# Token matmuls of one class in 64-lane pairs, and a new order in the head of a spectral and gated-GELU kernel

## The chip, the core and the metric

The kernel runs on one core of one Trainium2 chip. The metric is device time in microseconds, the median of several runs. An execution's time is a little longer than its span, which goes from the first to the last instruction of the trace.

## The reference

The rows of x (2048 rows of 512) are normalized. Two branches read the result and both are added to x. Branch A is a spectral filter: a two-dimensional real FFT over rows and columns, a product with complex weights (2048 x 257), and the inverse. Branch B is a gated feed-forward network: gelu(xn Wg) * (xn Wu), then Wd.

```python
def _A_ref(x, w_r, w_i):
    X = rfft2(x.astype(float32)) * (w_r + 1j * w_i)
    return irfft2(X, s=(S, D)).astype(bfloat16)

def _B_ref(x, w_gate, w_up, w_down):      # 512 -> 1792 -> 512
    g = jnp.einsum("bsd,df->bsf", x, w_gate)
    u = jnp.einsum("bsd,df->bsf", x, w_up)
    return jnp.einsum("bsf,fd->bsd", _gelu(g) * u, w_down)

xn = _layernorm(x, axis=-1)
return x + _A_ref(xn, A_w_r, A_w_i) + _B_ref(xn, B_w_gate, B_w_up, B_w_down)
```

## The kernel before, in words

**The planner.** No order is written by hand. Every operation is put on record with an engine, a cost in microseconds, what it reads and writes, PSUM or SBUF slots that it takes from pools, and a key. `_Sched.run` then places them one by one: it looks for the operation that can start earliest on any engine (ties by ready time plus key, or by a `due` time), and among those of the same engine that can start within 0.05 us (`SLACK`) takes the one with the lowest ready time plus key. For DMAs it keeps one transfer queue (`pipe`) with a rate of 340 GB/s. A TensorE operation of the spectral branch that becomes ready after 12 us is planned 1.0 us later than ready (`MARGIN`). The result is a fixed order for each of the five queues; `emit` writes it out with semaphore waits. On the chip every engine works strictly in that order, so an operation whose operand is late holds up all behind it on that engine.

**The head.** The 16 row tiles (128 rows each) are loaded by SyncE's queue, tiles 0 and 1 one by one, tiles 2 and 3 one by one behind a gate (`gate`, a warm matmul that must be over), and then in fours between the column blocks of Wg and Wu. The first 384 columns of Wg and Wu come through ACT's queue, columns 384 to 768 through SyncE's behind row tile 3. Meanwhile TensorE runs `warm` matmuls (L476) on a tile of zeros that DVE sets (L470). For a row tile, `stats` (L520, L521) gives mean and variance on DVE, `root_act` (square root on ACT L525, reciprocal on DVE L527) or `root_pool` (L532, L533, two tiles at once) the scale, `norm` (L537) the normalized tile, and `turn` transposes it on TensorE (L550) and copies it on DVE (L555) to xnT. Tile 0 goes in two halves (`first_half`: L570, L567, L572). Tiles 4 to 15 are transposed by DMA (L576).

**The gated branch.** `first` (L737) multiplies tiles 0 and 1 apart for hidden chunks 0 to 2, as soon as each is there. `gated` (L718) does one hidden chunk of 128 for a block of rows: four matmuls for gate, four for up, then Gelu (L723) and Copy (L724) on ACT and their product (L725) on DVE to hT. The first chunks go in halves of 256 rows. `down` (L766) multiplies hT with Wd. These operations are the filler of TensorE, in a fixed order.

**The spectral branch.** Four blocks of four row tiles: `mirror` makes the sequence's mirrored part (its transpose by TensorE for block 0, by DMA L592 for the others, into `odd`), `fold` the sums and differences (L613 to L621; L617 is the first that reads `odd`), then matmuls along columns (L631). The rest runs over tokens: butterflies on DVE to H (up to L842), token matmuls for eight classes v (L851; class 0, which has four with half their constants zero, L854), evacuation on ACT to X (L859), the product with the filter on DVE (L884 to L916, with the small columns of `edge` made by POOL at L864 and used at L898), and the way back (L931, L932, L991). The filter is loaded by 31 small DMAs on SyncE's queue.

Of the kernel before, what the change touches and what calls it, by code (L numbers as in the profile page):

```python
# [15 lines left out]
P = 128  # L16
NFC = 14
NHALF = 6
NFIRST = 3
WARM = 8  # L20
HKEY = 1.5
NORM = 14.0, 1.5
STAT = 13.0, 1.2
# [116 lines left out]
class _Op:  # L140
    __slots__ = ("eng", "fn", "cost", "key", "lag", "reads", "writes", "preds", "tiles", "first", "end", "pos", "dma", "seq",
                 "extra", "due")


class _Sched:
# [10 lines left out]

    def op(self, eng, cost, fn, reads=(), writes=(), tiles=(), key=0.0, after=(), dma=0, lag=0.0, due=None):
        o = _Op()
        o.eng, o.fn, o.cost, o.key, o.dma, o.lag, o.due = eng, fn, cost, key, dma, lag, due
# [41 lines left out]
    def run(self):  # L201
# [15 lines left out]
        while todo:  # L217
# [131 lines left out]
def bass_parallel_sum__spectral_gfnet__glu_gated_geglu__prompt_kernel(  # L349
# [24 lines left out]
    with ExitStack() as es:  # L374
# [29 lines left out]
        t2 = sb("edge2", [2, 4, 2])  # L404
        zero = sb("zero", [512])
        eps = sb("eps", [1], F32)
# [52 lines left out]

        def dma(q, dst, src, nbytes, wr=None, rd=None, key=0.0, after=(), cost=0.41, lag=0.0):  # L460
            after = tuple(after) + tuple(gate if q == "sp" else ())
            return op(q, cost, lambda e: e.dma_start(dst() if callable(dst) else dst.ap, src() if callable(src) else src.ap),
                      reads=rd if rd is not None else (), writes=wr if wr is not None else (), dma=nbytes, key=key, after=after, lag=lag)

# [4 lines left out]

        op("dve", 0.2, lambda e: e.memset(zero.ap, 0.0), writes=(zero,), key=-90)  # L470


        wt = _T("dn")

        def warm(key):
            return op("pe", 0.427, lambda e: e.matmul(ps_dn[:, :], zero.ap[:, 0:P], zero.ap, start=True, stop=True), reads=(zero,), tiles=(wt,), key=key)  # L476

        warms = [warm(-50) for _ in range(WARM)]


# [6 lines left out]
        k = iter(np.arange(0.0, 1.0, 0.001))  # L487
        def rows(lo, hi):
            return load("sp", x[:, lo:hi], xb[:, lo:hi, :], (hi - lo) * 131072, key=next(k))
# [32 lines left out]

        def root_act(s0, n, key):
# [3 lines left out]
            op("dve", 0.09, lambda e: e.reciprocal(rs.ap[:, sl], rs.ap[:, sl]), reads=(rs[:, sl],), writes=(rs[:, sl],), key=key)  # L527

# [54 lines left out]

        odd = {}

# [21 lines left out]
        def fold(b):  # L607
# [31 lines left out]
        stats(0, -60.0)  # L639
        stats(1, -55.0, None, (sch.ops[-1],))  # L640
        root_act(0, 1, -60.0)
        root_act(1, 1, -58.0)
        op("act", 1.5, lambda e: e.activation(tmp.ap, eps.ap, ACT.Gelu_apprx_tanh), reads=(eps, rs[:, 0:2]), writes=(tmp,), key=-30.0)
        for h in range(2):
            first_half(h)
        for s in range(2):
            if s:
                norm(s, -60.0)
                turn(s, 1, -60.0)
            warm(-30)  # L650
            if s == 0:
                stats(2, -30.0, None, (sch.ops[-2],))
        stats(3, -30.0, None, (sch.ops[-2],))
        root_pool(2, 2, -50.0)
        for s in (2, 3):
            norm(s, -50.0)
            turn(s, 1, -50.0)
        mirror(0)
        fold(0)
        for s in range(4, 16):  # L660
            stats(s, 0.0, STAT[0] + STAT[1] * (s - 4))
            if s % 2 == 1:
                root_pool(s - 1, 2, -4.0)
        hold = {}
        for s in range(4, 16):
# [3 lines left out]
            if s % 4 == 3:  # L669
                mirror(s // 4)  # L670
                hold[16] = sch.ops[-2]
                fold(s // 4)
# [370 lines left out]
```

## Time and profile before

| | |
|---|---|
| median of 3 runs | 172.11 us (172.04 to 172.81) |
| profiled execution | 172.02 us, its span 170.0 us |
| TensorE busy | 166.2 us, 998 matmuls |
| VectorE (DVE) busy | 146.1 us |
| ScalarE (ACT) busy | 106.0 us |
| GpSimd (POOL) busy | 11.5 us |
| DMA | 15.62 MB, 92 GB/s over the span |

In the profile PE is TensorE's matmuls and PEld its weight loads. A line such as L718 is a line of the kernel; since the planner sets the order, lines of one function are spread over the whole span. In rows of groups and of the timeline the bracket names the idle time before and what ended it. The rows of the chain give start, length and what ran. A matmul's listed length is longer than its slot, since matmuls overlap.

### The profile page before, as it was taken

The page shows a single profiled execution, that of the slowest core. Times are in us where ns is not written, and L with a number is a line of the kernel's source. Part 1 is how long each engine was busy: PE and PEld are TensorE (multiplying, and loading weights), DVE is VectorE, ACT ScalarE, POOL GpSimd, SP SyncE. Part 2 cuts the span into 40 slices and gives each one's busy share as a digit, 9 for nine tenths or more (in the row PEclk, how much of TensorE's full clock was granted, in tenths as well). Part 3 has the DMA queues.
Part 4 walks back from the last instruction along what each step waited for, and adds up shares of the span by engine and source line. Part 5 has one row for each costly group of instructions (what it writes and reads, how often), then busy time and mean ns, then how long its engine had stood idle before and what let it go on. Part 6 is the DMA issues. An engine that isn't in the chain of part 4 may idle for free.

```text
span 170.0 us, 2695 instructions
## 1 busy us (share of the span) xinstructions
PE 166.2 (98%) x998; PEld 85.9 (51%) x998; DVE 146.1 (86%) x295; ACT 106.0 (62%) x173; POOL 11.5 (7%) x23
## 2 busy tenths in 40 slices
PE   7999999999999999999999999999999999999994
PEld 2588544445556444444444465554445664444453
DVE  2879999796945999999999999999999969963931
ACT  3478776573977758588854696795637896561000
POOL 2022242500000000400000000000000000000000
DMA  5999989974975435000000000000000002300321
GB/s 145 344 346 348 277 176 327 189 211 83 121 128 125 85 53 198 0 6 0 0 0 0 0 4 0 0 0 0 4 0 2 0 4 99 128 19 0 123 68 62
DMA packets 22239, 15.62 MB, mean 92 GB/s; under 512 B 9165, under 2 KB 21714, under 8 KB 22226
## 3 DMA queue, kind: packets, MB, share of 16 engines
q1 hardware_dynamic: 21026, 14.60, 38.0%
q10 hardware_dynamic: 1200, 0.85, 1.6%
q8 instruction: 8, 0.13, 0.3%
q14 instruction: 5, 0.04, 0.1%
HBM read 11.38 MB, written 2.10 MB: 79 GB/s over the span
## 4 chain that ended last, share of the span: by engine, by line
PE 95%; DMA 3%; DVE 1%; issue 0%; DVEq 0%
PE ps_gu L718 55%; PE ps_dn L766 21%; PE ps_sp L766 7%; DMA x_sb<-in_A_x_dram 3%; PE ps_sp L631 2%; PE ps_sp L991 2%; PE ps_sp L851 2%; PE ps_sp L931 1%; PE ps_sp L932 1%; PE ps_dn L476 1%; PE ps_gu L737 1%; PE ps_sp L854 1%; DVE bst L520 0%; PE ps_dn L737 0%; PE ps_sp L550 0%; DVE xnT L555 0%
## 5 line engine op out<-in xcount | busy, mean ns | idle before, releaser
L718 PE MATMUL ps_gu<-xnT,wg 128*128 128x512 bf16 (+1 forms) x236 | 56.7, 363 | 0.0
L718 PE MATMUL ps_gu<-xnT,wu 128*128 128x512 bf16 (+1 forms) x236 | 56.7, 363 | 0.0
L723 ACT ACTIVATE gg<-ps_gu 128x512 bf16<-128x512 f32 (+1 forms) x59 | 33.7, 571 | 14.3 <-PE ps_gu L718 12.1
L724 ACT ACTIVATE uu<-ps_gu 128x512 bf16<-128x512 f32 (+1 forms) x59 | 33.9, 574 | 10.5 <-PE ps_gu L718 10.2
L766 PE MATMUL ps_dn<-wd,hT 128*128 128x512 bf16 x168 | 39.0, 379 | 0.0
L466 DVE TENSOR_TENSOR specB<-specB 128x512 bf16<-128x512 bf16 (+2 forms) x58 | 33.1, 609 | 3.8 <-DMA specB<-specB 2.3
L718 PEld LDWEIGHTS ps_gu<-xnT,wu 128*128 128x128 bf16 x236 | 22.8, 98 | 23.2
L718 PEld LDWEIGHTS ps_gu<-xnT,wg 128*128 128x128 bf16 x236 | 22.6, 98 | 22.3 <-ACT uu L752 0.2
L766 PEld LDWEIGHTS ps_dn<-wd,hT 128*128 128x128 bf16 x168 | 16.2, 98 | 18.6
L725 DVE TENSOR_TENSOR hT<-gg,uu 128x512 bf16<-128x512 bf16 (+1 forms) x59 | 22.6, 393 | 1.7 <-ACT uu L724 1.6
L774 ACT ACTIVATE db<-ps_dn 128x512 bf16<-128x512 f32 x12 | 7.2, 597 | 17.7 <-PE ps_dn L766 17.7
L520 DVE BATCH_NORM_STATS2 bst<-x_sb 128x6 f32<-128x512 bf16 x16 | 10.9, 684 | 2.6 <-DMA x_sb<-in_A_x_dram 2.6
L466 DVE TENSOR_TENSOR specC<-specB 128x1024 bf16<-128x1024 bf16 (+2 forms) x18 | 12.4, 712 | 0.2
L766 PE MATMUL ps_sp<-wd,hT 128*128 128x512 bf16 (+2 forms) x70 | 12.3, 336 | 0.0
L466 DVE TENSOR_TENSOR specB<-specA 128x2048 bf16<-128x2048 bf16 x8 | 9.4, 1217 | 1.4 <-ACT specA L636 1.4
L466 DVE TENSOR_TENSOR specB<-specB,filt 128x2048 bf16<-128x2048 bf16 x8 | 9.4, 1219 | 0.0
L766 PEld LDWEIGHTS ps_sp<-wd,hT 128*128 128x128 bf16 x70 | 6.3, 98 | 6.1 <-DVE x_sb L777 0.2
L775 DVE TENSOR_TENSOR x_sb<-db,x_sb 128x512 bf16<-128x512 bf16 x12 | 5.0, 418 | 4.8 <-ACT db L774 4.7
L859 ACT ACTIVATE specA<-ps_sp 128x1024 bf16<-128x1024 f32 x8 | 8.0, 1035 | 1.5 <-PE ps_sp L851 1.3
L996 ACT ACTIVATE specB<-ps_sp 128x1024 bf16<-128x1024 f32 x8 | 7.8, 1031 | 0.4 <-PE ps_sp L991 0.4
L937 ACT ACTIVATE specC<-ps_sp 128x1024 bf16<-128x1024 f32 x8 | 7.8, 1034 | 0.3 <-PE ps_sp L932 0.3
L636 ACT ACTIVATE specA<-ps_sp 128x1024 bf16<-128x1024 f32 x8 | 7.8, 1031 | 0.0
(71 smaller groups left out, 128.9 us busy)
## 6 DMA issues: line engine op xcount, KB each, us to landing
out_dram<-x_sb SPq DMA_DIRECT2D x15, 128.0 KB, 1.8
wd<-in_B_w_down_dram SPq DMA_DIRECT2D x1, 1792.0 KB, 8.7
x_sb<-in_A_x_dram SPq DMA_DIRECT2D x3, 512.0 KB, 8.5
wg<-in_B_w_gate_dram SPq DMA_DIRECT2D x2, 512.0 KB, 8.7
wu<-in_B_w_up_dram SPq DMA_DIRECT2D x2, 512.0 KB, 9.2
toki<-c_ti SPq DMA_DIRECT2D x1, 768.0 KB, 4.7
tokf<-c_tf SPq DMA_DIRECT2D x1, 576.0 KB, 4.4
x_sb<-in_A_x_dram SPq DMA_DIRECT2D x4, 128.0 KB, 3.6
```

The source lines that it names most:

```text
L466: return op("dve", c_tt(n), lambda e: e.tensor_tensor(o.ap, a.ap, b.ap, f), reads=(a, b), writes=(o,), key=key, **kw)
L520: op("dve", 0.61, lambda e: e.bn_stats(bst[:, s].ap, xs(s).ap), reads=(xs(s),), writes=(bst[:, s],), key=key, due=due, after=after)
L636: op("act", c_act(1024), lambda e, yv=yv, t=t: e.activation(yv.ap, spair(t).rearrange("p (s r i) -> p s i r", s=4, r=4), ACT.Copy), writes ...
L718: ins = e.matmul(gub(t, n), w.ap[:, dc, fc * P:(fc + 1) * P], xnT.ap[:, b, sl, dc, :], start=(dc == 0), stop=(dc == 3))
L723: op("act", c_act(n), lambda e: e.activation(gg.ap[:, gs.slot, 0:n], gub(g, n), ACT.Gelu_apprx_tanh), tiles=(g, gs), key=0.0)
L724: op("act", c_act(n), lambda e: e.activation(uu.ap[:, us.slot, 0:n], gub(u, n), ACT.Copy), tiles=(u, us), key=0.0)
L725: op("dve", c_tt(n), lambda e: e.tensor_tensor(hT.ap[:, h.slot, lo:lo + n], gg.ap[:, gs.slot, 0:n], uu.ap[:, us.slot, 0:n], MUL), tiles=(g ...
L766: ins = e.matmul(bank(), hT.ap[:, hs[(b, fc)].slot, sl * P:(sl + 1) * P], wd.ap[:, fc, lo:lo + n], start=(fc == 0), stop=(fc == NFC - 1))
L774: op("act", c_act(n), lambda e: e.activation(db.ap[:, d.slot, 0:n], bank(), ACT.Copy), tiles=(t, d), key=0.0)
L859: op("act", c_act(1024), lambda e, xv=xv, t=t: e.activation(xv.ap, spair(t), ACT.Copy), writes=(xv,), tiles=(t,), key=-0.5)
L937: op("act", c_act(1024), lambda e, gv=gv, t=t: e.activation(gv.ap, spair(t).rearrange("p (k x i) -> p k x i", k=4, x=4), ACT.Copy), writes ...
L996: op("act", c_act(1024), lambda e, rv=rv, t=t: e.activation(rv.ap, spair(t), ACT.Copy), writes=(rv,), tiles=(t,), key=-0.5)
```

## The change

It has five parts.

1. Class 0 of the token stage: instead of four matmuls over 128 lanes, with constants of which half are zero, four over 64 lanes, two on the lower and two on the upper lanes, each kind into its own bank. The planner's cost for it goes from four matmuls to two.
2. The warm matmuls read a constant of ones that the runtime sets, not a tile that DVE sets. There are ten of 512 and one of 256 columns at the start, where there were eight and two more later. The gate for row tiles 2 and 3 is the fourth instead of the third.
3. In the head, the two copies of tile 0 go from DVE to ACT, and the Gelu dummy that loads its table waits for them. Statistics of tiles 2 and 3 come after the copy of tile 1. The roots of tiles 2 and 3 on POOL are made one by one. The first reciprocal is ordered behind the second statistics, and statistics of tiles 4 to 15 behind norm 3.
4. The planner gets fixed landing times (`land`) for the first columns of Wg and Wu and for row tiles 2 and 3, which then take no time in its transfer queue. NORM, the due time of the norms, goes from 14.0 to 15.0.
5. The filter loads wait for the operation at L617 of block 3, which reads the last mirrored transpose, instead of for the one that makes that transpose's source.

```diff
-WARM = 8
+WARM = 10 * (512,) + (256,)
-NORM = 14.0, 1.5
+NORM = 15.0, 1.5
...
-            if o.dma:
+            if o.land:
+                o.end = o.land
+            elif o.dma:
                 pipe = max(pipe, st + 1.9) + o.dma / RATE
...
-        op("dve", 0.2, lambda e: e.memset(zero.ap, 0.0), writes=(zero,), key=-90)
+        ones = nc.const_aps.tensor(1.0, (P, 512), BF16)
-        def warm(key):
-            return op("pe", 0.427, lambda e: e.matmul(ps_dn[:, :], zero.ap[:, 0:P], zero.ap, start=True, stop=True), reads=(zero,), tiles=(wt,), key=key)
+        def warm(n):
+            return op("pe", 0.000834 * n, lambda e: e.matmul(ps_dn[:, 0:n], ones[:, 0:P], ones[:, 0:n], start=True, stop=True), tiles=(wt,), key=-50)
...
-            wload("act", w, v, 0, 384, key=0.5)
+            wload("act", w, v, 0, 384, key=0.5, land=5.5 if w is wg else 6.4)
-        gate.append(warms[2])
+        gate.append(warms[3])
         for i in (2, 3):
-            rows(i, i + 1)
+            rows(i, i + 1, 6.3 + 0.3 * i)
...
-            op("dve", 0.21, lambda e: e.tensor_copy(o.ap, bank()), writes=(o,), tiles=(t,), key=-70.0)
+            op("act", 0.27, lambda e: e.activation(o.ap, bank(), ACT.Copy), writes=(o,), tiles=(t,), key=-70.0)
...
             tt(f[:, :, 2], f[:, :, 3], odd[b], SUB, 512, kk)
+            turned[b] = sch.ops[-1]
...
         stats(0, -60.0)
-        stats(1, -55.0, None, (sch.ops[-1],))
-        root_act(0, 1, -60.0)
-        root_act(1, 1, -58.0)
-        op("act", 1.5, lambda e: e.activation(tmp.ap, eps.ap, ACT.Gelu_apprx_tanh), reads=(eps, rs[:, 0:2]), writes=(tmp,), key=-30.0)
+        stats(1, -66.0, None, (sch.ops[-1],))
+        root_act(0, 1, -75.0, (sch.ops[-2],))
+        root_act(1, 1, -64.0)
         for h in range(2):
             first_half(h)
-        for s in range(2):
-            if s:
-                norm(s, -60.0)
-                turn(s, 1, -60.0)
-            warm(-30)
-            if s == 0:
-                stats(2, -30.0, None, (sch.ops[-2],))
-        stats(3, -30.0, None, (sch.ops[-2],))
-        root_pool(2, 2, -50.0)
+        op("act", 1.5, lambda e: e.activation(tmp.ap, eps.ap, ACT.Gelu_apprx_tanh), reads=(eps, xnT[:, 0, 0], rs[:, 0:2]), writes=(tmp,), key=-30.0)
+        norm(1, -60.0)
+        turn(1, 1, -60.0)
         for s in (2, 3):
+            stats(s, -58.0, None, (sch.ops[-1],))
+        for s in (2, 3):
+            root_pool(s, 1, -50.0)
             norm(s, -50.0)
+            early = sch.ops[-1]
             turn(s, 1, -50.0)
...
-            stats(s, 0.0, STAT[0] + STAT[1] * (s - 4))
+            stats(s, 0.0, STAT[0] + STAT[1] * (s - 4), (early,))
...
-        gate.append(hold[16])
+        gate.append(turned[3])
...
-                for r in range(2):
-                    if v:
-                        ins = e.matmul(spb(t, r), tf.ap[:, 2 + 2 * v + r], H.ap[:, hh[r]], start=True, stop=True)
-                    else:
-                        for i in range(2):
-                            ins = e.matmul(spb(t, r), tf.ap[:, 2 * r + i], H.ap[:, hh[i]], start=(i == 0), stop=(i == 1))
+                for r in range(2) if v else ():
+                    ins = e.matmul(spb(t, r), tf.ap[:, 2 + 2 * v + r], H.ap[:, hh[r]], start=True, stop=True)
+                for i in range(0 if v else 2):
+                    for r in range(2):
+                        l = slice(64 * r, 64 * r + 64)
+                        ins = e.matmul(spb(t, r), tf.ap[l, 2 * r + i], H.ap[l, hh[i]], start=(i == 0), stop=(i == 1))
                 return ins
-            op("pe", (2 if v else 4) * mm(512), f_t, reads=(H[:, hh[0]], H[:, hh[1]], tf), tiles=(t,), lag=0.1)
+            op("pe", 2 * mm(512), f_t, reads=(H[:, hh[0]], H[:, hh[1]], tf), tiles=(t,), lag=0.1)
```

More of the change, by code (lines that the diff above doesn't have):

```diff
@@ L141 @@
     __slots__ = ("eng", "fn", "cost", "key", "lag", "reads", "writes", "preds", "tiles", "first", "end", "pos", "dma", "seq",
-                 "extra", "due")
+                 "extra", "due", "land")
 class _Sched:
@@ L155, in pool, with op @@
         self.pools[name] = n
-    def op(self, eng, cost, fn, reads=(), writes=(), tiles=(), key=0.0, after=(), dma=0, lag=0.0, due=None):
+    def op(self, eng, cost, fn, reads=(), writes=(), tiles=(), key=0.0, after=(), dma=0, lag=0.0, due=None, land=None):
         o = _Op()
-        o.eng, o.fn, o.cost, o.key, o.dma, o.lag, o.due = eng, fn, cost, key, dma, lag, due
+        o.eng, o.fn, o.cost, o.key, o.dma, o.lag, o.due, o.land = eng, fn, cost, key, dma, lag, due, land
         o.reads, o.writes, o.tiles = reads, writes, [(t, False) for t in tiles]
@@ L404, in bass_parallel_sum__spectral_gfnet__glu_gated_geglu__prompt_kernel @@
         t2 = sb("edge2", [2, 4, 2])
-        zero = sb("zero", [512])
         eps = sb("eps", [1], F32)
@@ L458, in bass_parallel_sum__spectral_gfnet__glu_gated_geglu__prompt_kernel, with dma @@
         gate = []
-        def dma(q, dst, src, nbytes, wr=None, rd=None, key=0.0, after=(), cost=0.41, lag=0.0):
+        def dma(q, dst, src, nbytes, wr=None, rd=None, key=0.0, after=(), cost=0.41, lag=0.0, land=None):
             after = tuple(after) + tuple(gate if q == "sp" else ())
             return op(q, cost, lambda e: e.dma_start(dst() if callable(dst) else dst.ap, src() if callable(src) else src.ap),
-                      reads=rd if rd is not None else (), writes=wr if wr is not None else (), dma=nbytes, key=key, after=after, lag=lag)
+                      reads=rd if rd is not None else (), writes=wr if wr is not None else (), dma=nbytes, key=key, after=after, lag=lag, land=land)
         def tt(o, a, b, f, n, key=0.0, **kw):
@@ L468, in bass_parallel_sum__spectral_gfnet__glu_gated_geglu__prompt_kernel @@
         ADD, SUB, MUL = ALU.add, ALU.subtract, ALU.mult
-        op("dve", 0.2, lambda e: e.memset(zero.ap, 0.0), writes=(zero,), key=-90)
+        ones = nc.const_aps.tensor(1.0, (P, 512), BF16)
         wt = _T("dn")
-        def warm(key):
-            return op("pe", 0.427, lambda e: e.matmul(ps_dn[:, :], zero.ap[:, 0:P], zero.ap, start=True, stop=True), reads=(zero,), tiles=(wt,), key=key)
-        warms = [warm(-50) for _ in range(WARM)]
+        def warm(n):
+            return op("pe", 0.000834 * n, lambda e: e.matmul(ps_dn[:, 0:n], ones[:, 0:P], ones[:, 0:n], start=True, stop=True), tiles=(wt,), key=-50)
+        warms = [warm(n) for n in WARM]
         def load(q, dst, src, nbytes, **kw):
@@ L487, in bass_parallel_sum__spectral_gfnet__glu_gated_geglu__prompt_kernel, with rows @@
         k = iter(np.arange(0.0, 1.0, 0.001))
-        def rows(lo, hi):
-            return load("sp", x[:, lo:hi], xb[:, lo:hi, :], (hi - lo) * 131072, key=next(k))
+        def rows(lo, hi, land=None):
+            return load("sp", x[:, lo:hi], xb[:, lo:hi, :], (hi - lo) * 131072, key=next(k), land=land)
         load("act", small[:, 0:2].rs([2 * P]), c_small.ap()[:, 0:2 * P], 65536, key=-9)
         for w, v in ((wg, wgv), (wu, wuv)):
-            wload("act", w, v, 0, 384, key=0.5)
+            wload("act", w, v, 0, 384, key=0.5, land=5.5 if w is wg else 6.4)
         rows(0, 1)
         rows(1, 2)
-        gate.append(warms[2])
+        gate.append(warms[3])
         for i in (2, 3):
-            rows(i, i + 1)
+            rows(i, i + 1, 6.3 + 0.3 * i)
         for w, v in ((wg, wgv), (wu, wuv)):
@@ L521, in stats, with root_act @@
             op("dve", 0.11, lambda e: e.bn_aggr(bag[:, s].ap, bst[:, s].ap), reads=(bst[:, s],), writes=(bag[:, s],), key=key, due=due)
-        def root_act(s0, n, key):
+        def root_act(s0, n, key, after=()):
             sl = slice(s0, s0 + n)
@@ L526, in root_act @@
                reads=(bag[:, sl], eps), writes=(rs[:, sl],), key=key)
-            op("dve", 0.09, lambda e: e.reciprocal(rs.ap[:, sl], rs.ap[:, sl]), reads=(rs[:, sl],), writes=(rs[:, sl],), key=key)
+            op("dve", 0.09, lambda e: e.reciprocal(rs.ap[:, sl], rs.ap[:, sl]), reads=(rs[:, sl],), writes=(rs[:, sl],), key=key, after=after)
         def root_pool(s0, n, key):
@@ L582, in bass_parallel_sum__spectral_gfnet__glu_gated_geglu__prompt_kernel @@
         z = R3(0, [16, 4, P])
-        odd = {}
+        odd, turned = {}, {}
         def mirror(b):
@@ L670, in bass_parallel_sum__spectral_gfnet__glu_gated_geglu__prompt_kernel @@
                 mirror(s // 4)
-                hold[16] = sch.ops[-2]
                 fold(s // 4)
```

## The prediction

> **What bounds the kernel now.** I read the page first: the busy times, then the chain that ended last.
>
> ```profile
> PE 166.2 (98%) x998; PEld 85.9 (51%) x998; DVE 146.1 (86%) x295; ACT 106.0 (62%) x173; POOL 11.5 (7%) x23
> PE 95%; DMA 3%; DVE 1%; issue 0%; DVEq 0%
> ```
>
> TensorE is the bound from the first real matmul to the last. From the groups' rhythm (0.2157 us per 512-wide matmul: 14 in 3.02; 0.109 at 256; 0.056 at 128) I add up what it must stream after its first L737 matmul at 6.11: 160.7 us. Its last stream ends at about 167.55 (167.71 less the 163 ns by which a matmul's 379 ns exceed its 216 ns slot). So 167.55 - 6.11 - 160.7 = some 0.8 us is all that TensorE loses after 6.11. No edit can win more there, except by taking stream time away. Next the chain in order of time, to see where the 0.8 lies:
>
> ```profile
> 1.17 1.48 PE ps_dn L476 x3
> ...
> 2.67 4.26 DMA x_sb<-in_A_x_dram
> ...
> 7.01 0.69 DVE bst L520
> 7.71 0.33 DVE xnT L555
> ...
> 8.09 1.07 PE ps_gu L737 x16
> ```
>
> Statistics of row tile 2 stand in DVE's queue ahead of the copy that brings row tile 1 to xnT, and wait for their rows until 7.01; TensorE sits 0.26 us before 8.09. With 0.15 between the halves of tile 0 (the first two matmuls end their slots at 6.22, the next start at 6.37), that is half of the loss. Third, weight loads and DMA landings just behind it:
>
> ```profile
> 9.38 0.37 PEld L718 LDWEIGHTS ps_gu<-xnT,wg 128*128 128x128 bf16 x4
> 9.89 0.13 PEld L718 LDWEIGHTS ps_gu<-xnT,wu 128*128 128x128 bf16 x2
> ```
> ```profile
> wu<-in_B_w_up_dram SPq DMA_DIRECT2D x1, 384.0 KB, 5.8
> ```
>
> The weight load of a group normally begins with the last matmul of the group before, here 9.77. This one came at 9.89. The wu columns 384 to 768, issued at 3.99, land 5.8 later, at 9.8, and 0.08 is what lies between landing and use elsewhere (row tile 2: landing 6.92, use 7.01). So chunk 3's up matmul already waits for DMA, for 0.04 of matmul time, while the DMA engines run at 330 to 360 GB/s from 3.3 on. **That landing is a wall for everything the head gains before it.** Last, the middle, where filter loads are moved:
>
> ```profile
> 49.78 0.88 DVE L466 TENSOR_TENSOR specB<-specB 128x512 bf16<-128x512 bf16 x2 [2.25 <-DMA specB<-specB]
> ```
> ```profile
> 68.29 2.12 POOL L864 TENSOR_TENSOR edge<-filt 128x16 bf16<-128x16 bf16 x2 [35.41 <-DMA filt<-in_A_w_r_dram]
> ```
> ```profile
> 76.14 0.26 DVE L898 TENSOR_TENSOR edge<-specA,edge 128x16 bf16<-128x16 bf16 x2
> ```
>
> The edge columns are ready at 70.41 and used at 76.14: 5.7 us of slack.
>
> **The change part by part.**
>
> *Token stage of class 0 (L854).* Four 128-lane matmuls become four of 64 lanes, in two pairs on different lanes and banks. The chain has the four at 0.86 us. If a pair runs side by side, two slots go: -0.43. The trace has no matmul over 64 lanes, so the other bound is: nothing overlaps, and TensorE empties at the change to 64 lanes and back, twice the 163 ns by which a matmul outlasts its slot: +0.33. I take -0.30: the pairs overlap, less one emptying of 0.13 to 0.16. The Trainium skill, "TensorEngine Tiling (Array Packing)", Tiling Modes, Key Properties, speaks against the change here: changing the tiling mode drains TensorE, though tiles of one mode run in parallel. By that rule, with the drain's length from the 163 ns above, the part is worth -0.43 + 0.33 = -0.10; no run here shows it yet. ACT, which waits for this bank (L859 waits 0.2 for L854), has spare time.
>
> *Warming.* DVE's memset (0.27) goes and the warm matmuls need no wait: they start at about 0.75 to 0.85, where SyncE and DVE start, not 1.17. Ten and a half at 0.427 end by 5.3; the last one before was already short (0.40 against 0.63), so the array was at speed at 4.99. The first transposes waited for L570 until 5.44 and still do: worth 0. The gate for row tiles 2 and 3 moves from the third warm matmul to the fourth: 0.8 + 4 x 0.427 + 0.2 = 2.7, against 2.67. Nothing moves.
>
> *Copies of tile 0 on ACT.* DVE does one in 0.29, ACT reads 256 columns in 0.38 (L751): +0.09 on the start, 6.11 to 6.20. The table load for Gelu, 1.28, moves behind them, from 5.50 to about 6.45, ends with its dummy by 7.95, and its cover is the wait before 8.74 (1.75 idle, 0.7 left). Unknown is whether Copy right after Sqrt needs a table of its own; the trace has Gelu and Copy alternating 59 times without a load. The bounds are 0 and one more load of 1.28, which less the 0.34 of room before the wall (below) costs 0.94. I take 0. The Trainium skill, "ScalarE: Activation LUTs", Table sets, has Copy in every set, so no load; for the square root's set no run shows it.
>
> *Order in the head.* The reciprocal goes behind the second L520, where it ran already (4.85 after 4.24): 0. DVE, free of two copies (0.57), does norm 1 at 5.7 rather than 6.23; its transposes follow at 6.31, its xnT copy ends by 7.2 rather than 8.04. Tile 0 and the transposes take TensorE 6.20 + 0.11 + 0.22 + 22 x 0.056 = 7.77, tile 1 (24 x 0.056) to 9.11, chunk 3's gate matmuls to 9.55. So 0.34 us is won up to there. Then comes the up matmul and the landing at 9.8: it starts at 9.89 to 9.92, as before. By the planner's own costs (taken for the order only) transposes of tile 2 are ready 0.11 after TensorE is free, over its window of 0.05, so they stay behind this matmul and cannot fill the hole. What remains: 0.04 at the wall is not won, 0.07 at the next group (waiting for L752) and 0.03 before the mirror's transposes are, since ACT runs earlier: -0.10. Statistics 2 and 3 end near 8.0 and 8.8, one root each on POOL (0.22 + 0.71 at most, for two before), norms by 10.3: early enough.
>
> *Landing times, NORM.* They alter the plan alone. Fixed landings no longer count in the planner's transfer queue, so later loads look some 1.4 us earlier than before. Used first are x rows 4 to 7 (real 11.2, statistics at 12.37), 8 to 11 (15.8, 18.94), 12 to 15 (22.0, 24.53): 1.2 us or more of room each. Worth 0.
>
> *Filter loads gated on L617 of block 3.* The 31 loads leave SyncE's queue ahead of the last mirror transpose (two at 40.55 did), which lands without them; DVE's wait of 2.25 goes, L617 runs at 46.3 to 47.5, and the spectral chain behind it comes 2.3 to 3.2 earlier. The loads start there, not at 40.55. From 43.10 to the last landing at 68.29 they took 25.2, with the first two (1.2) 26.4, perhaps 2 less without the transpose among them. So the edges are ready at 46.3 + 24.4 + 2.1 = 72.8 to 47.5 + 26.4 + 2.1 = 76.0, the middle 74.4. DVE reaches L898 at 72.9 to 73.9. **The slack of 5.7 is gone, and DVE may wait 0 to 3 us, likeliest 0.9.** Behind it are H's last three sums and the multiplies of hidden tiles; TensorE waits for the sums at L851 (78.27; they end at about 77.5, after 76.32 + 1.15) and has 0.8 of room there, up to half a group (0.4) more. So 0.9 costs TensorE nothing, 3 costs about 2.
>
> *Sum.* Profiled execution: 172.02 = span 170.0 + 2.02 around it. -0.30 - 0.10 + 0 = -0.40: 171.62. The median of the runs is 0.09 above the profiled one: 171.7.
>
> **Rivals.**
>
> *A, the wall is not there.* If the weights land 0.35 sooner, the head's 0.34 and the 0.10 stay, with -0.43 from the pairs: 0.9 off, 171.2. For it: the loads behind are interleaved with these, so the landing can shift. Against: 330 to 360 GB/s from 3.3 on leaves no hole to close, and the issue times do not move.
>
> *B, slower: the filter loads take the place of the transpose wait.* DVE stands at L898 for edges that L864 has not made. It decides once the edges come over 1.2 after DVE is there, and TensorE then loses the rest one for one: at 3 late 1.8, less 0.4 won, 173.5; at 2.5 late 173.0. For it: 5.7 of slack taken from both ends. Against: the middle of my bounds is 0.9 late.
>
> *C, the pairs win nothing.* Drains or no overlap: -0.10 to +0.33 with -0.10 from the head, 171.9 to 172.3.
>
> *D, another table load for Copy.* +0.94 - 0.30: 172.75.
>
> **How the numbers follow.** A measurement here can tell about 0.5%, 0.86 us. Forecast 0.52, its own range 171.3 to 172.0 (the pairs from -0.43 to 0, small waits of a new order of 0.3); A 0.16; B 0.16; C 0.13; D 0.03. Faster by 0.86 are two thirds of A (0.11; it lies just at the bound) and the end of the forecast (0.05), if the 0.2 us that TensorE loses elsewhere goes as well: 0.16. Slower are half of B (0.08; a wait over 2.5) and what of the forecast, C and D meets a late operand somewhere in the new order (0.08): 0.16. The rest, 0.68, is no change. The range takes in A with those 0.2 (171.0), C, D, and B up to a wait of 2.3 (172.8).
>
> **What would show it.** Right: the up matmul of chunk 3 still at 9.9 with TensorE idle for some 0.3 before it, and the one at 8.09 at about 7.8; the four L854 matmuls starting in two pairs, with their span near 0.55; no DVE wait for specB near 49; L864 ending at 73 to 76. Wrong: chunk 3's up matmul at 9.6 (A); a DVE wait at L898 and a TensorE gap before L851 (B); L854 starts 216 ns apart, or gaps of 160 ns around them (C); three table loads (D). A TensorE wait anywhere after 12 that none of this names would break the sum.

## The result and the profile after

The changed kernel takes 171.58 us (median of 22 runs, 171.24 to 174.14), the kernel before 172.16 beside it (22 runs, 171.66 to 172.81). The ratio is 0.9971, with an interval of 0.996 to 0.9982: 0.3% faster, which the interval tells from no change, but less than the 0.5% that was named as the bound. One of the 22 runs, that of 174.14, had a mean granted clock of 0.99 where the others had 1.0, and is left out of the ratio. Twelve more runs in a later session gave 171.44 against 172.08, ratio 0.9972 (0.9954 to 0.9991). The profiled execution took 171.33 us, with a span of 169.5. The prediction was 171.7, and no change.

From the page of the kernel after, the busy times and the engines' shares of the chain:

```profile
PE 166.0 (98%) x999; PEld 86.1 (51%) x999; DVE 146.0 (86%) x292; ACT 106.6 (63%) x175; POOL 11.3 (7%) x25
PE 95%; DMA 2%; DVE 1%; ACT 0%; issue 0%
```

Nothing has changed hands: TensorE is the bound from its first real matmul to the last. Its chain in order of time (start, length, what), head, class 0 and end. The names are the same, most line numbers are 3 lower (L718 is now L715, L737 L734, L854 L851, L851 L847, L864 L861, L898 L895):

```profile
3.35 0.70 DVE bst L520
...
6.05 0.39 ACT xnT L572
...
6.49 0.29 PE ps_gu L734 x2
...
63.54 0.43 PE ps_sp L847 x2
63.97 0.54 PE ps_sp L851 x4
64.51 5.29 PE ps_gu L715 x24
...
155.14 12.14 PE ps_sp L763 x70
```

The start slipped from 6.11 to 6.49, class 0 takes 0.54 instead of 0.86, and the last stream ends at 167.27 instead of 167.71: 0.44 earlier, where 0.40 was summed up. The agreement hides that the terms are not those of the sum, as the experiments show. The timeline of TensorE in the head:

```profile
9.40 0.60 PE L715 MATMUL ps_gu<-xnT,wg 128*128 128x256 bf16 x4
9.84 0.60 PE L715 MATMUL ps_gu<-xnT,wu 128*128 128x256 bf16 x4
```

The second row is chunk 3's up matmul, in front of which 0.3 us of idle time was forecast. There is none: it starts in its slot, 0.44 after the gate matmuls. And the middle, groups on POOL and DVE from the timeline:

```profile
74.13 0.67 POOL L861 TENSOR_TENSOR edge<-filt 128x16 bf16<-128x16 bf16 x2 [42.15 <-DMA filt<-in_A_w_r_dram]
```
```profile
74.61 0.41 DVE L895 TENSOR_TENSOR edge<-specA,edge 128x16 bf16<-128x16 bf16 x2 [0.19 <-POOL edge L861]
```

The edge columns are ready 4.4 us later than before, DVE starts its sums with them 1.5 earlier, and the slack of 5.7 has become a wait of 0.19.

### The profile page after: what moved, and what is told of

Same layout as the page of the kernel before. It is cut to its first block, busy times and chain, and to the rows that moved or that the text cites. A ratio compares the mean times of both kernels' runs of the same rounds, so it can differ in the third digit from the quotient of the medians.

```text
span 169.5 us, 2696 instructions
## 1 busy us (share of the span) xinstructions
PE 166.0 (98%) x999; PEld 86.1 (51%) x999; DVE 146.0 (86%) x292; ACT 106.6 (63%) x175; POOL 11.3 (7%) x25
## 4 chain that ended last, share of the span: by engine, by line
PE 95%; DMA 2%; DVE 1%; ACT 0%; issue 0%
PE ps_gu L715 56%; PE ps_dn L763 21%; PE ps_sp L763 7%; PE ps_sp L988 2%; PE ps_sp L632 2%; PE ps_sp L847 2%; DMA x_sb<-in_A_x_dram 2%; PE ps_gu L734 1%; PE ps_sp L928 1%; PE ps_sp L929 1%; DVE bst L520 1%; PE ps_dn L734 1%; PE ps_sp L550 0%; PE ps_sp L851 0%; PE ps_sp L567 0%; ACT xnT L572 0%
## 5 line engine op out<-in xcount | busy, mean ns | idle before, releaser
L715 PE MATMUL ps_gu<-xnT,wg 128*128 128x512 bf16 (+1 forms) x236 | 56.7, 363 | 0.0
L715 PE MATMUL ps_gu<-xnT,wu 128*128 128x512 bf16 (+1 forms) x236 | 56.7, 363 | 0.0
L467 DVE TENSOR_TENSOR specB<-specB 128x512 bf16<-128x512 bf16 (+2 forms) x58 | 33.6, 610 | 1.7 <-ACT specB L993 1.4
L715 PEld LDWEIGHTS ps_gu<-xnT,wu 128*128 128x128 bf16 x236 | 22.9, 98 | 23.0
L715 PEld LDWEIGHTS ps_gu<-xnT,wg 128*128 128x128 bf16 x236 | 22.6, 98 | 22.0 <-ACT uu L721 0.4
L520 DVE BATCH_NORM_STATS2 bst<-x_sb 128x6 f32<-128x512 bf16 x16 | 11.0, 686 | 3.4 <-DMA x_sb<-in_A_x_dram 3.3
```

Source lines behind the costliest of these rows:

```text
L467: return op("dve", c_tt(n), lambda e: e.tensor_tensor(o.ap, a.ap, b.ap, f), reads=(a, b), writes=(o,), key=key, **kw)
L520: op("dve", 0.61, lambda e: e.bn_stats(bst[:, s].ap, xs(s).ap), reads=(xs(s),), writes=(bst[:, s],), key=key, due=due, after=after)
L715: ins = e.matmul(gub(t, n), w.ap[:, dc, fc * P:(fc + 1) * P], xnT.ap[:, b, sl, dc, :], start=(dc == 0), stop=(dc == 3))
```

## The experiments

Two measures are used throughout, since the medians tell few of these kernels apart and a gain of 0.2 us is small against what the head differs by from one execution to the next: the start of chunk 3's up matmul ("up"), and the end of TensorE's last stream minus that start ("rest"). In the kernel before they are 9.92 and 157.79, in the profiled execution after 9.84 and 157.43. Single times and spans are those of one profiled execution.

| kernel | up | rest | time, us |
|---|---|---|---|
| before | 9.92 | 157.79 | 172.16 |
| pairs_only | 9.90 | 157.61 | 172.01 (ratio 0.9993, 0.998 to 1.0007) |
| after | 9.84 | 157.43 | 171.58 (0.9971, 0.996 to 0.9982) |
| after_again | 10.06 | 157.43 | 171.44 (0.9972, 0.9954 to 0.9991) |
| no_pairs | 10.07 | 157.65 | 171.77, one run |
| same_lanes | 10.39 | 157.43 | 171.87, one run |
| all_lower | 10.34 | 157.86 | 172.24, one run |
| recip_free | 9.95 | 157.43 | 171.78, one run |
| early_chunk3 | 9.58 | 157.44 | 171.53 (0.9971, 0.9958 to 0.9984) |
| gate_old | 9.96 | 157.44 | 171.54, one run |
| edge_mild | 9.90 | 159.35 | 173.30, one run |
| edge_late | 11.50 | 161.84 | 177.38, one run |
| best | 9.61 | 158.26 | 171.85 (0.9993, 0.9977 to 1.001) |

### The pairs alone, and everything but the pairs

*pairs_only*: the kernel before with only the new matmuls of class 0, at the old planned cost so that the order stays.

```diff
-                for r in range(2):
-                    if v: ...
-                    else:
-                        for i in range(2):
-                            ins = e.matmul(spb(t, r), tf.ap[:, 2 * r + i], H.ap[:, hh[i]], ...)
+                for r in range(2) if v else ():
+                    ins = ...                        # as before
+                for i in range(0 if v else 2):
+                    for r in range(2):
+                        l = slice(64 * r, 64 * r + 64)
+                        ins = e.matmul(spb(t, r), tf.ap[l, 2 * r + i], H.ap[l, hh[i]], ...)
```

> The kernel before with only the 64-lane pairs; the planner's costs stay, so every queue keeps its order. Theory (pairs worth 0.22 on TensorE, head the other 0.20): class 0 takes 0.64 from the end of the slot ahead to the next group's start instead of 0.863, the last down matmul ends 0.22 earlier, at 167.49 instead of 167.71, span 169.8, time about 171.9, ratio 0.9987. Rival 1 (what the pairs save is given back where TensorE waits for DVE later): the end stays at 167.7. Rival 2 (the pairs make the whole gain, the head none): the end at 167.3. The head stays as before: first L737 at 6.11, chunk 3's up matmul at 9.92.

*no_pairs*: the kernel after, with that hunk undone.

> The changed kernel with the four full-array matmuls of class 0 again, order unchanged. Theory: class 0 takes 0.863, the last down matmul ends at 167.28 + 0.22 = 167.50, span 169.7. If the pairs were worth nothing at the end it would stay at 167.3; if they made the whole gain, 167.7. It also is one more sample of the head: whether the transposes at L567 run at the slow clock (288 ns each) or at the full one (224), and whether chunk 3's up matmul starts right behind its gate matmuls (landing not binding) or at landing + 0.08.

Class 0 in the chain of pairs_only, and then of no_pairs:

```profile
65.94 0.54 PE ps_sp L854 x4
66.48 3.56 PE ps_gu L718 x16
```
```profile
64.20 0.86 PE ps_sp L851 x4
65.07 4.96 PE ps_gu L715 x23
```

In the timeline the slot before class 0 ends at 63.81 in the kernel after, the first pair starts at 63.90, the second at 64.13, the next group of 128 lanes at 64.44, and its second matmul 0.01 later than a slot: 0.64 in all, where four matmuls took 0.86. That is 0.22. The rest agrees: 0.18 less in pairs_only than before, 0.22 more in no_pairs than after. The pairs are the larger half of the 0.36 that the kernel gained behind the head. The median of pairs_only alone could not show it: its interval takes in no change.

### What the 0.64 is made of

*same_lanes*: the kernel after with the two loops exchanged, so that the two matmuls over the lower lanes come first and those over the upper lanes behind them.

```diff
-                for i in range(0 if v else 2):
-                    for r in range(2):
+                for r in range(0 if v else 2):
+                    for i in range(2):
```

> The changed kernel with the same four 64-lane matmuls, but both of the lower lanes first, then both of the upper. Theory (two matmuls run side by side only when neighbours in the queue stand on different lanes): only the second and third overlap, three slots of 0.216 and two changes of 0.10, 0.85 from slot end to the next group, so the last down matmul ends at about 167.5. Rival (the array overlaps any, or 64-lane matmuls are themselves faster): 0.64 and 167.3. Rival (nothing overlaps here): 1.06 and 167.7.

*all_lower*: all four on the lower lanes; the upper half's products are left out.

```diff
-                        l = slice(64 * r, 64 * r + 64)
+                        l = slice(0, 64)
```

> The changed kernel with all four 64-lane matmuls of class 0 on the lower lanes, so the second bank holds the lower lanes' sums and the upper half's work is left out. Theory 1 (matmuls on different lanes run side by side, in whatever order they are queued, as same_lanes suggests): with one set of lanes nothing can overlap, four slots of 0.216 and two changes of 0.10, 1.06 from slot end to the next group, the end 0.42 later than with pairs. Theory 2 (a 64-lane matmul takes half a slot by itself): 0.64 as with pairs.

Class 0 in the chain of same_lanes, its first matmuls in the timeline, and the chain of all_lower:

```profile
64.52 0.54 PE ps_sp L851 x4
65.06 5.07 PE ps_gu L715 x23
```
```profile
64.45 0.39 PE L851 MATMUL ps_sp<-specC,tokf 64*128 64x512 bf16 x2
```
```profile
64.47 0.97 PE ps_sp L851 x4
65.43 4.64 PE ps_gu L715 x21
```

On the same lanes the four stand one behind the other: from the end of the slot before (64.30) to the next group (65.37) it is 1.07 us, counted in the same way, and the rest is longer by 0.43, two slots. So on different lanes the pairs overlap wholly, and 0.64 - 2 x 0.2157 = 0.21 is what going to 64 lanes and back costs, about 0.10 each way. The idea that neighbours in the queue must lie on different lanes fell: with the lower lanes' two first the same 0.54 came out, and two of the four start together at 64.45 and two some 0.2 later. The trace does not say which two, but since all_lower shows that matmuls on the same lanes don't overlap, each pair must be one of the lower and one of the upper lanes. So a matmul on free lanes seems not to wait behind one that waits for its own, and what was said of the kernel before, that every engine works strictly in its queue's order, would then not hold to the letter for TensorE. The Trainium skill, "TensorE: Matmul & The Clock Gate", Part 3, The mechanism, has matmuls start and end in the order of the program; these starts do not agree with that.

### The reciprocal's order and the wall

*recip_free*: the kernel after without the ordering of the first reciprocal behind the second statistics.

```diff
-        root_act(0, 1, -75.0, (sch.ops[-2],))
+        root_act(0, 1, -75.0)
```

> The changed kernel without the order of the first reciprocal behind the second statistics; the queues of the head keep their order, only the wait goes. Theory (that wait on DVE's own statistics is the 0.12 by which the first halves come later, 5.22 - 5.07 less 0.05 for a later landing): L570 starts at about 5.1 (1.75 after the first statistics instead of 1.87), L567 at 5.5 instead of 5.62, the first L734 at 6.37, chunk 3's up matmul at 9.72 unless the landing of wu (about 9.6, + 0.08) stands in the way, the end at 167.15. Rival (DVE finishes the statistics before the reciprocal anyway): L570 1.87 after the first statistics, nothing moves.

The timeline of recip_free, and the same row of the second execution of the kernel after:

```profile
9.12 0.60 PE L715 MATMUL ps_gu<-xnT,wg 128*128 128x256 bf16 x4
9.95 0.60 PE L715 MATMUL ps_gu<-xnT,wu 128*128 128x256 bf16 x4 [0.23 <-DMA wu<-in_B_w_up_dram]
```
```profile
10.06 0.60 PE L715 MATMUL ps_gu<-xnT,wu 128*128 128x256 bf16 x4 [0.24 <-DMA wu<-in_B_w_up_dram]
```

Without the ordering DVE reaches L570 1.78 after the first statistics began, with it 1.87 (both executions of the kernel after), in the kernel before 1.77. The first real matmul comes at 6.20 and tile 1 at 7.78, the numbers of the prediction, and then the wall is there: TensorE could go on at 9.56 and starts at 9.95, because the wu columns land 5.8 after their issue at 3.98. no_pairs shows the same wait (10.07, with gate matmuls at 9.27). In the first execution after they landed 5.6 after issue, at 9.60, and TensorE was not free before 9.84. So the wall stands, and what stood before it was merely later by the slow start.

The wall also explains most of the column "up" in the table. Taken from the traces to the hundredth, landing and start are 9.79 and 9.92 in the kernel before, 9.81 and 9.95 in recip_free, 9.94 and 10.07 in no_pairs, 9.93 and 10.06 in after_again, 9.83 and 9.96 in gate_old, 10.25 and 10.39 in same_lanes, 10.20 and 10.34 in all_lower: 0.13 to 0.14 each time. (The prediction took 0.08 for it, from another load.) In the other executions TensorE was not free until later than that. The rows of gate_old and all_lower name an operation of ACT as what ended the wait, but in the kernel after the same matmul starts at 9.84, before those two operations of ACT end.

### The wall taken away

*early_chunk3*: recip_free, with columns 384 to 512 of Wg and Wu in loads of their own ahead of columns 512 to 768.

```diff
-        for w, v in ((wg, wgv), (wu, wuv)):
-            wload("sp", w, v, 384, 768, key=next(k))
+        for lo, hi in ((384, 512), (512, 768)):
+            for w, v in ((wg, wgv), (wu, wuv)):
+                wload("sp", w, v, lo, hi, key=next(k))
```

> The changed kernel without the wait of the first reciprocal, and with columns 384 to 512 of Wg and Wu (chunk 3) in two loads of their own ahead of 512 to 768. Theory (the landing of wu columns 384 to 768, at 9.6 to 10.3 in the runs so far, is the wall; in recip_free TensorE stood from 9.56 to 9.95 for it): chunk 3's up matmul starts right behind its gate matmuls, at about 9.56, and the last down matmul ends 157.43 later, at 167.0; span 169.25, time about 171.3, ratio 0.995. Chunk 4's columns are wanted at 10.2 and 10.65, the wall moves there and may keep up to 0.2. Rival (the wait is for something else, or the two small loads slow the queue so that chunk 4 waits as long as chunk 3 did): end at 167.3 to 167.4 as in recip_free.

The same row of the timeline:

```profile
9.58 0.60 PE L716 MATMUL ps_gu<-xnT,wu 128*128 128x256 bf16 x4
```

The small load lands 4.4 after issue and the wait is gone: up starts 0.37 earlier than in recip_free, and since the rest is the same, the end of the profiled execution is the earliest of all, 167.02. In the median 0.05 less than the kernel after in its first session and 0.09 more than in its second: with intervals of 0.2 to 0.3 us on either side, the times cannot tell these two apart.

Their spans can, in part. The record has the span of every run, and its median is 169.3 in early_chunk3, 169.75 and 169.55 in the two sessions of the kernel after, 170.1 in the kernel before. But the time around the span differs too, from kernel to kernel and hardly from session to session: its median is 2.01 to 2.04 before (three sessions), 1.85 and 1.84 after, 2.00 in pairs_only, 1.87 in best, and 2.18 in early_chunk3, which loses there about what its head gains. Nothing in the traces shows where this time goes.

### The filter loads

*gate_old*: the kernel after with the filter loads waiting, as before, for the operation that makes the last transpose's source.

```diff
-        gate.append(turned[3])
+        gate.append(hold[16])
```

> The changed kernel with the filter loads gated as before, on the source of the last mirror transpose. Theory (the middle is worth nothing to TensorE, whose loss lies in the head): DVE waits some 2 us for the transpose near 49 again, the edges are ready at 70 to 72 instead of 74.8, the small products at L895 come 1.5 to 2 later, and TensorE's last down matmul still ends 157.43 after the start of chunk 3's up matmul. Rival (the later gate is part of the gain): that distance grows by 0.1 or more.

POOL and DVE of gate_old:

```profile
69.35 1.15 POOL L862 TENSOR_TENSOR edge<-filt 128x16 bf16<-128x16 bf16 x2 [37.25 <-DMA filt<-in_A_w_r_dram]
```
```profile
47.37 0.88 DVE L467 TENSOR_TENSOR specB<-specB 128x512 bf16<-128x512 bf16 x2
74.46 0.26 DVE L896 TENSOR_TENSOR edge<-specA,edge 128x16 bf16<-128x16 bf16 x2
```

The loads start at 42.42, the edges are ready at 70.50, 4.0 before their use, and yet DVE's wait of 2.25 at 47 does not come back: in the new plan the last transpose stands ahead of all the loads (at 41.11) without the new gate. The wait went with the other parts of the change; which of them did it was not separated. The gate brings nothing here, and it spends the slack.

*edge_late* and *edge_mild* price a shortage of that slack: a load that nothing reads, of 0.92 or 0.52 MB, stands ahead of the filter loads.

```diff
         gate.append(turned[3])
+        load("sp", scratch, wdv[:, 0:7], 7 * 131072, key=next(k), land=60.0)
```

> The changed kernel with one more load of 0.92 MB to a spare tile ahead of the filter loads (planned at no time), so that the edges come some 2.7 later, at 77.4 instead of 74.8. Theory (my rival B's price): DVE stands 2.7 to 2.9 us at L895, TensorE loses what is over 1.2 of it, about 1.6, ahead of the next L847 matmuls, and the end moves as much: 159.0 after the start of chunk 3's up matmul, against 157.43. Rival (TensorE has more room, the room of hidden tiles between them included): it moves by less than 0.5.

> The kernel after with 0.52 MB (four of the seven parts of the 0.92 MB) loaded ahead of the filter loads into a tile that nothing reads. With 0.92 MB the edges came 3.3 us later, DVE stood 3.48 us at the edge sums, TensorE 2.51 before L849, and then ran 3.42 us at half its clock. Scaled by 4/7: edges 1.9 later, DVE stands 0.2 + 1.9 = 2.1, TensorE 2.1 - 0.97 = 1.1. Theory 'one for one': the end moves by 1.1 and the clock stays at 1.0. Rival 'any idle time of TensorE of about a microsecond costs the clock': 1.7 more, 2.8 in all, with granted clock 0.5 for some 3.4 us behind the wait. A third outcome, no wait before L849: the room behind L897 is larger than 0.97. The head's start is a draw of up to 1.7 us and is taken out by end minus start of chunk 3's up matmul, 157.43 in the kernel after.

From edge_late the timelines of DVE and TensorE, then two windows of one microsecond (window, its length, busy time of PE, PEld, DVE, ACT and POOL, then the granted clock, the DMA share and GB/s):

```profile
79.56 0.18 DVE L897 TENSOR_TENSOR edge<-specA,edge 128x16 bf16<-128x16 bf16 x1 [3.48 <-POOL edge L863]
```
```profile
81.30 1.64 PE L849 MATMUL ps_sp<-specC,tokf 128*128 128x512 bf16 x4 [2.51 <-DVE specC L468]
82.73 1.91 PE L717 MATMUL ps_gu<-xnT,wg 128*128 128x512 bf16 x4
```
```profile
83.00:84.00 1.00, 1.00 (x3) 0.29 (x2) 1.00 (x2) 1.00 (x2) 0.00 (x0) 0.50 0.00 0
85.00:86.00 1.00, 1.00 (x6) 0.41 (x5) 1.00 (x3) 0.46 (x2) 0.00 (x0) 0.96 0.00 0
```

The rest grew by 4.41. 2.67 of it is the wait, counted from the end of one slot to the next start (the row's 2.51 leaves out the 0.16 by which a listed matmul outlasts its slot). The clock fell to half at 81.66, 0.36 after TensorE had started again, and stayed there for 3.41 us, which cost 1.71. Together that is 4.38. The Trainium skill, "TensorE: Matmul & The Clock Gate", HAM oscillation, gives "no PE-idle gaps >~3.4µs" as the rule; here, in one execution, a gap of 2.51 was enough. DVE and TensorE of edge_mild:

```profile
76.53 0.18 DVE L897 TENSOR_TENSOR edge<-specA,edge 128x16 bf16<-128x16 bf16 x1 [2.04 <-POOL edge L863]
```
```profile
78.28 1.21 PE L849 MATMUL ps_sp<-specC,tokf 128*128 128x512 bf16 x4 [1.08 <-DVE specC L468]
108.82 0.23 PE L930 MATMUL ps_sp<-toki,specA 128*128 128x128 bf16 x1 [0.24 <-DVE specA L897]
```

DVE stood 2.04 and 0.20, TensorE 1.08 at L849 as expected, and the clock stayed at 1.0. But the rest grew by 1.92, not by 1.1: neither theory had it. From slot to slot TensorE lost 1.24 before the first of the four at L849 and another 0.16 before the third, which waits for DVE's next sum: 1.40 there. The other 0.5 was lost further on, 0.10 before the matmuls at 98.42 and 0.40 before those at 108.82. DVE is busy for 31.88 of the 32 us from 78 to 110 in the kernel after, so it never makes up what it lost, and TensorE comes upon it again. The kernel after at the second place:

```profile
106.31 0.36 DVE L895 TENSOR_TENSOR specA<-edge 128x8 bf16<-128x8 bf16 x3
```
```profile
106.84 0.22 PE L928 MATMUL ps_sp<-toki,specA 128*128 128x128 bf16 x1
```

DVE is done at 106.67. Where TensorE waits for it, it starts 0.05 behind (108.77 and 108.82 in edge_mild), so the room is 0.84 - 0.67 - 0.05 = 0.12 us. In the kernel before DVE is done at 108.15 with this group, and TensorE comes to it at 109.00: room of 0.8.

### Putting the parts together

*best*: early_chunk3, the two copies of tile 0 back on DVE, the filter loads gated as before. *after_again*: the kernel after, in the same session. Of best's edit only the copies are shown:

```diff
-            op("act", 0.27, lambda e: e.activation(o.ap, bank(), ACT.Copy), ...)
+            op("dve", 0.21, lambda e: e.tensor_copy(o.ap, bank()), ...)
```

> The parts that paid, without those that did not: the kernel after without the reciprocal's ordering, columns 384 to 512 of Wg and Wu in loads of their own, the two copies of tile 0 on DVE, and the filter loads gated as before. Theory: against the version with the early columns alone (171.53, up matmul at 9.58) the copies give 0.10 at the start and the gate nothing: 171.4, up matmul at 9.5, edges ready near 70.5 and DVE at them near 74.4. Rival, that copies on DVE push tile 1's norm back and TensorE waits for tile 1 as in the kernel before: up matmul 9.6 to 9.9, 171.5 to 171.8.

> The kernel after once more, on the chip and among the runs of the two others: 171.6 as before (0.9971 of the kernel before). Theory: the head varies by draw (clock rise 4.1 to 6.5 us, landing of the wu columns 9.6 to 10.3), so chunk 3's up matmul starts anywhere from 9.8 to 10.4, and end minus that start stays 157.43. Rival, that the 9.84 of its first profile is the rule: 9.84 again with no wait for DMA before it.

DVE and TensorE of best, just behind the head:

```profile
12.20 0.70 DVE L521 BATCH_NORM_STATS2 bst<-x_sb 128x6 f32<-128x512 bf16 x1 [0.24 <-DMA x_sb<-in_A_x_dram]
12.81 0.41 DVE L556 COPY xnT<-ps_sp 128x512 bf16<-128x512 bf16 x1
```
```profile
13.28 0.61 PE L717 MATMUL ps_gu<-xnT,wg 128*128 128x256 bf16 x4 [0.54 <-DVE xnT L556]
```

The copies did give their 0.09 (L567 to the first L734, here L568 to L736: 0.67, against 0.76 in after_again), but TensorE then stands 0.13 between the two halves of tile 0, until 6.37, as it did in the kernel before, while with the copies on ACT tile 1's transposes filled that place. So up starts at 9.61, no earlier than in early_chunk3. The wall has moved on by one chunk: the next wu columns land at 10.68 and are used at 10.82, 0.11 after TensorE was free. But the planner laid the rest out anew: the statistics of row tile 4 stand in DVE's queue ahead of the copy of an earlier tile's transposes, wait for their rows until 12.20, and TensorE loses 0.7 before 13.28 from slot to slot. It is the pattern of the kernel before at 7.01, one step on. 171.85 is 0.4 above the 171.44 of the kernel after in the same session: not a version to keep. after_again has the rest of 157.43 again and the wall, as the theory said and not as its rival. No version tried is measurably faster than the change as it was made.

## Why the prediction was right

**The pairs** (-0.30 taken): mechanism right, size off, -0.22. The overlap is whole, as taken; the mis-sized term is the emptying, "one of 0.13 to 0.16", which is two of 0.10. The Trainium skill's rule ("TensorEngine Tiling (Array Packing)", Tiling Modes, Key Properties) agrees in kind, a drain at each change; it was the length of 0.163, from a matmul's listed length, that made -0.10 of it. Rival C is out: no_pairs and all_lower both show the gain.

**Warming, copies and the reciprocal** (start at 6.20): wrong. In the profiled execution the first real matmul came at 6.49, 0.38 later than before instead of 0.09. Of this 0.05 is the first rows' landing, 0.10 the reciprocal, 0.09 the copies on ACT as predicted, 0.03 the step from L570 to L567, and 0.11 the transposes, which ran at the low clock (0.28 to 0.31 listed for each, against 0.22 to 0.23), because it rose later than in the kernel before. The step that failed is "the reciprocal goes behind the second L520, where it ran already: 0". It did run behind it, but at 4.85, in the tail of the 0.69 that the statistics are listed with; told to wait, it starts at 5.02, 0.73 after their start instead of 0.61. The "worth 0" of warming holds for the gain, but its "array was at speed" is a draw: in recip_free and after_again the transposes are fast, in pairs_only and edge_mild they are not.

**Rival D** is out. ACT's rows have one table load after the copies, at 6.72, as forecast, and none between the square roots and the copies (the one at 2.29 is for the square root):

```profile
6.05 0.66 ACT L572 ACTIVATE xnT<-ps_sp 128x256 bf16<-128x256 bf16 x2 [0.46 <-PE ps_sp L567]
6.72 1.28 ACT L646 ACT_TABLE_LOAD   x1
```

The Trainium skill's rule that every set holds Copy ("ScalarE: Activation LUTs", Table sets) agrees here for the set of the square root too.

**The wall** (up at 9.89 to 9.92 whatever the head gains): right as a mechanism, by the six later executions that run into it (recip_free, no_pairs, after_again, gate_old, same_lanes, all_lower), and by early_chunk3, which takes it away. The place of the wall is not fixed: it moves with the landing, from 9.92 to 10.39 in the executions that met it. The marks given for it did not all show in the first profile: tile 1 without a wait, but at 8.06 and not at 7.8, and no idle time ahead of the up matmul, because the start had eaten 0.29 of the 0.34. The sum was robust to this error, since the wall makes the head's gain worthless either way: start and wall together gave 0.08, where 0 was summed up, and this 0.08 is within what the landing varies by (up at 9.84 and 10.06 in the two executions; in the second the last stream ends at 167.49, 0.22 earlier than before and not 0.44).

**Rival A** (171.2): the weights did land 0.2 sooner in the first execution, and it was no use, as TensorE was later. Its price holds roughly: early_chunk3 has up 0.37 earlier than recip_free. The median of 171.53 does not show it, as the time around its span is longer by 0.33.

**Order behind the wall** (-0.10): 0.36 of rest less 0.18 to 0.22 for the pairs, so 0.14 to 0.18. 0.12 lies before 12.45, close to the rows that were named; the few hundredths behind were not located.

**The filter loads**: the times were right, edges at 74.8 in a range of 72.8 to 76.0 with its middle at 74.4, a DVE wait of 0.19 in 0 to 3. The forecast of no cost came true, but by luck in part. "So 0.9 costs TensorE nothing" is the step that failed: the room of 1.2 was read at the first place where TensorE meets DVE, where edge_mild bears it out nearly (2.24 late, 1.24 lost from slot to slot, so 1.0), and not at the later ones. At L928 it is 0.12 in the new order, so by these numbers a wait of 0.9 instead of 0.19 would have cost some 0.6 (an estimate). **Rival B** was therefore priced too low: 2.24 of waiting cost 1.92 and not 1.0, and at 3.68 the clock's fall was added, 4.41 in all. And the reason given for the end of the 2.25 wait, the new gate, is not it, by gate_old.

The sum of -0.40 met -0.44 in the trace: pairs -0.22, order -0.14, start of the up matmul -0.08. That they agree so closely is in part luck: the pairs gave 0.08 less than summed up, and the order and a landing that came 0.19 earlier made up for it. Of the median's -0.58 the remaining 0.14 is not in the chain. The sum took the 2.02 around the span as fixed, without a reason; over all runs its median is 2.01 to 2.04 before and 1.84 to 1.85 after. So almost 0.2 of the gain lies outside everything that the sum counts, and why was not found.

## What to carry to other kernels

Halves of a matmul whose constants are half zero can run side by side on separate lanes, but two slots saved cost half of themselves again in the change of lanes and back, so the fewer such changes the better. When slack is spent on an engine that is nearly as busy as the bound, look for the narrowest place where the bound meets it until it next idles, not for the first. Idle time between listed matmuls is short by the 0.16 that a matmul outlasts its slot, so what a wait costs is better counted from slot to slot. And an ordering that states what already happens is not free where it turns an overlap of 0.1 us at the end of an operation into a wait.

## What the runs showed of the hardware

- Two 64-lane matmuls on different lanes overlap wholly in both orders of the queue that were run (0.64 for four either way, 1.07 on the same lanes), and the change from 128 to 64 lanes, and back, leaves 0.10 us each.
- The clock fell after a gap of 2.51 us of TensorE and not after one of 1.08 (one execution each); the fall came after the gap, 3.0 us behind the last slot before it, and lasted 3.41 us at half speed.
- The matmul that needs a load's columns started 0.13 to 0.14 us after the landing in all seven executions in which chunk 3's up matmul waited for it, and in best for the chunk after.
- The rise of the clock in the head is a draw. The same eleven warm matmuls, from 0.76 on, took 3.82 to 4.64 us; in after_again the clock rose at about 3.6, 2.8 after the first of them. In edge_late the clock was low, by the length of the matmuls, until 10.0, and up was 1.66 later than in the kernel after, although the column of the granted clock shows 1.00 there. TensorE's timeline in edge_late, two groups of the same form:

```profile
9.47 0.63 PE L736 MATMUL ps_gu<-xnT,wg 128*128 128x128 bf16 x4
10.17 0.39 PE L736 MATMUL ps_gu<-xnT,wg 128*128 128x128 bf16 x4
```

The Trainium skill, "TensorE: Matmul & The Clock Gate", Part 1, has the gate watch a free-running window of some 3.4 us; that the rise differs from run to run agrees, but 10.0 is 9.2 us after the first warm matmul, with TensorE idle for only 0.24 and 0.44 us in between (at 5.40 and 6.07).
